# Packed attention in eight array tiles: four heads of 64 rows by 32 columns in place of two pairs of 128 by 64

## The chip, the cores and the metric

The kernel runs on one core of one Trainium2 chip. The metric is the device time of one execution in microseconds, lower is better. A core has TensorE (matmuls into PSUM, an array of 128 rows by 128 columns), VectorE (DVE in the rows), ScalarE (ACT), GpSimd (POOL) and SyncE (SP), which here issues the DMA transfers. PE in the rows is a matmul on TensorE, PEld the load of its stationary operand.

## The reference, cut to what matters

Three layers run in a row on 8 batches of 576 tokens. The change is in the first, a packed attention with 8 heads of 64 features: 32 packed queries `p` attend to the 576 keys and values, and the tokens' queries `q` then attend to the 32 packed values.

```python
def _attn_ref(q, k, v, p):                      # (8, 8, 576, 64), p: (8, 8, 32, 64)
    scale = 1.0 / np.sqrt(q.shape[-1])
    def sm_attn(qq, kk, vv):
        s = scale * np.matmul(qq, kk.transpose(0, 1, 3, 2))
        s = s - np.max(s, axis=-1, keepdims=True)
        a = np.exp(s)
        a = a / (np.sum(a, axis=-1, keepdims=True) + 1e-09)
        return np.matmul(a, vv)
    p_packed = sm_attn(p, k, v)                 # 32 packed values per head
    return sm_attn(q, p_packed, p_packed)
```

Its output `x` (576 x 512 per batch) goes into a mixture of four causal attention experts (`x @ wq[e]`, `x @ wk[e]`, `x @ wv[e]`, the two best experts by `x @ w_gate`), and that into a gated feed-forward layer (`r * (k * k @ w_v)` with `k = relu(xk @ w_k)`, `r = sigmoid(xr @ w_r)`).

## The kernel before, in words

The program has two parts in time. In the first, for each of the 8 batches, two *fronts* compute the packed attention of four heads each (`front(b, g)`, `g` in 0 and 1). The packed attention's output `x` itself is never formed: since `x` is the softmax weights (`A2`) times the packed values, the packed values are multiplied with the experts' weights first (`PW` = packed values times `wa`, 772 columns: queries, keys, values and gate of all experts). `project` and `values` then multiply `A2` and `PW`, each split into a high and a low part (`A2h`, `A2l`, `PWh`, `PWl`). `soft`, `turn` and `pair_out` are the causal attention of the experts. Between them run `fold` and `vweights`, which decode the last layer's weights on VectorE, ScalarE and GpSimd (lines L576 to L617) and multiply some of them on TensorE (L670). In the second part, from about 440 us on, TensorE runs the last layer (`rstage` L801, `kstage` L823, `vstage` L856).

In a front, four heads lie as two pairs. The packed queries of a pair stand in `pT` with zeros beside them (128 rows are two heads' features, 64 columns are two heads' queries, block diagonal), so that a matmul of 128 rows by 64 columns gives both heads' scores. Four such matmuls (two pairs, two halves of 288 tokens) are a call of `scores_pair`, L204, once with the keys `kT` and once with the queries `qT`. The product of weights and values is at L260 (five blocks of tokens, two pairs, 128 value columns), after which `bmask` puts zeros in the wrong head's place (L267). `PW` is at L290. The steps of a front in order are: loads (L223 to L235), key scores and their softmax (L204, L239 to L247), transposes of the weights (L251), product with the values (L260, L267), transposed packed values (L273), query scores (L204, L280 to L285), `PW` (L290 to L297), the rest of the softmax (L300 on) and `A2` (L307).

All matmuls of a front are in float32. Each is two passes in the trace, so a matmul in the program stands there as two loads and two matmul rows.

The order of the work is set twice. A table of due times (`FRONT_T`, `VAL_T`, `SOFT_T` and so on, in units in which a batch takes 20) sorts the pieces into one sequence, in which the generators are advanced. A scheduler then lays the instructions out on each engine by a simulated timeline and the priorities of `PR`. The change alters no due time, but the scheduler's result shifts with the instructions.

Of the kernel before, what the change touches and what calls it, by code (L numbers as in the profile page):

```python
# [9 lines left out]
F32 = mybir.dt.float32  # L10
# [40 lines left out]
def f32(ap):  # L51
    return ap.bitcast(F32)
# [3 lines left out]
def kernel(  # L56
# [3 lines left out]
):  # L60
    nc = tc.nc
    P = 128
    B, NG, _, _, S = q.shape
    D, NPK = p.shape[3], p.shape[5]
    DM, DFF = w_k.shape
    NE, HD = 4, wo.shape[1] // 4
    SH = S // 2
    NT = (S + P - 1) // P
    TAIL = S - (NT - 1) * P
    QB = 256  # L70
# [3 lines left out]
    NCB = S // NPK  # L74
    VG = HD * NE + NE
    NQK = QK + VG
    assert w_in.shape == (DM, NQK) and out.shape[2] == DM == NG * 4 * D
    assert (P, S, D, NPK, HD, NE, NT, TAIL) == (128, 576, 64, 32, 64, 4, 5, 64)
    SC = 1.0 / math.sqrt(D)

# [11 lines left out]
    def nm(s):  # L92
        uid[0] += 1
        return f"{s}_{uid[0]}"
# [12 lines left out]
        out=mstrip[:, 512:], in_=mstrip[:, 512:], pattern=[[-1, P]], base=0,  # L107
        channel_multiplier=1, compare_op=ALU.is_ge, fill=NEG,
    )
    bmask = const.tile([P, 2, D], F32, name="bmask")  # L110
    nc.vector.memset(bmask, 0.0)
    for h in range(4):
        nc.vector.memset(bmask[32 * h : 32 * h + 32, h % 2, :], 1.0)
    lower = const.tile([P, NE, NE], F32, name="lower")
    nc.vector.memset(lower, 0.0)
    for e in range(1, NE):
# [25 lines left out]
    if True:  # L142
# [6 lines left out]
        ex_cm, ex = pool("ex", 2, "left")  # L149
        bt_cm, bt = pool("bt", 1, "left")  # L150

        wa = wa_pool.tile([P, NDT, NQK], F32, name="wa")

# [3 lines left out]
        kls = [ex.tile([P, 2, S], F32R, name=f"kl{x}", bufs=1) for x in range(2)]  # L157
        mss = [ex.tile([P, S], F32, name=f"ms{x}", bufs=1) for x in range(6)]
        vns = [ld.tile([P, NT, 4 * D], F32, name=f"vn{x}", bufs=1) for x in range(2)]
        pTs = [fr.tile([P, P], F32, name=f"pT{x}", bufs=1) for x in range(2)]  # L160
        for t in pTs:
            nc.gpsimd.memset(t, 0.0)

# [14 lines left out]
                yield  # L178

        def load_wa():  # L180
            nc.sync.dma_start(wa, w_in.rearrange("(c p) n -> p c n", p=P))

        def halves(ap):
            return ap.rearrange("p (h n) -> p h n", h=2)
# [12 lines left out]
        def pool_tt(o, x, y, op):  # L197
            nc.gpsimd.tensor_tensor(o, x, y, op=op)  # L198

        def scores_pair(lhs, rhs):  # L200
            ps = big()
            for hf in range(2):
                for jj in range(2):
                    nc.tensor.matmul(  # L204
                        ps[64 * jj : 64 * jj + 64, 512 * hf : 512 * hf + SH],
                        lhs[:, 64 * jj : 64 * jj + 64],
                        rhs[:, jj, SH * hf : SH * hf + SH],
                        start=True, stop=True,
                    )
            return halves(ps)[:, :, :SH]  # L210

        def front(b, g):


            if g == 0:
                bats[b] = {
                    n_: bt.tile([P, NG, w], F32R, tag=n_, name=nm(n_))
                    for n_, w in (("A2h", S), ("A2l", S), ("PWh", NQK), ("PWl", NQK))
                }
            bat = bats[b]  # L220
            pT = pTs[(b * NG + g) % 2]
            for h in range(2):
                nc.sync.dma_start(  # L223
                    pT[64 * h : 64 * h + 64].rearrange("d (j h n) -> d j h n", j=2, h=2)[:, :, h, :],
                    p[b, g, h],
                )
            kT = ld.tile([P, 2, S], F32, tag="kT", name=nm("kT"))
            nc.sync.dma_start(kT, k[b, g])
            vn = vns[(b * NG + g) % 2]
            nc.sync.dma_start(  # L230
                vn[:, : NT - 1, :], v[b, g, : (NT - 1) * P].rearrange("(c p) x -> p c x", p=P)
            )
            nc.sync.dma_start(vn[TAIL:, NT - 1, :], v[b, g, (NT - 1) * P :])
            qT = ld.tile([P, 2, S], F32, tag="qT", name=nm("qT"))
            nc.sync.dma_start(qT, q[b, g])  # L235
            yield
            s1 = scores_pair(pT, kT)
            mx = sm.tile([P, 1], F32, tag="mx1", name=nm("mx1"))
            nc.vector.tensor_reduce(mx, s1, op=ALU.max, axis=AX.XY)  # L239
            nb = sm.tile([P, 1], F32, tag="nb1", name=nm("nb1"))  # L240
            nc.vector.tensor_scalar(nb, mx, -SC, None, op0=ALU.mult)
            a1 = fr.tile([P, S], F32, tag="sa", name=nm("a1"), bufs=4)
            su = sm.tile([P, 1], F32, tag="su1", name=nm("su1"))
            nc.scalar.activation(halves(a1), s1, AF.Exp, bias=nb, scale=SC, accum_out=su)
            nc.vector.tensor_scalar(su, su, EPS, None, op0=ALU.add)
            ri = sm.tile([P, 1], F32, tag="ri1", name=nm("ri1"))
            nc.vector.reciprocal(ri, su)  # L247
            yield
            ps = big()
            for c in range(NT):  # L250
                nc.tensor.transpose(  # L251
                    ps[:, c * P : (c + 1) * P], a1[:, start(c) : start(c) + P], ident
                )
            aT = fr.tile([P, NT, P], F32, tag="aT1", name=nm("aT1"), bufs=1)
            evac(E_AT, aT.rearrange("p c q -> p (c q)"), ps[:, : NT * P])
            yield
            ps = one()
            for c in range(NT):
                for jj in range(2):
                    nc.tensor.matmul(  # L260
                        ps[64 * jj : 64 * jj + 64, :P],
                        aT[:, c, 64 * jj : 64 * jj + 64],
                        vn[:, c, P * jj : P * jj + P],
                        start=c == 0, stop=c == NT - 1,
                    )
            pp = fr.tile([P, P], F32, tag="pp", name=nm("pp"))
            nc.vector.scalar_tensor_tensor(  # L267
                pp, ps[:, :P], ri, bmask.rearrange("p a d -> p (a d)"),
                op0=ALU.mult, op1=ALU.mult,
            )  # L270
            yield
            ps = one()
            nc.tensor.transpose(ps[:, :P], pp, ident)  # L273
            ppT = fr.tile([P, P], F32, tag="ppT", name=nm("ppT"))
            evac(E_PPT, ppT, ps[:, :P])
            yield
            s2 = scores_pair(ppT, qT)
            st = fr.tile([P, S], F32, tag="sa", name=nm("st"), bufs=4)
            for hf in range(2):
                nc.vector.transpose(st[:, SH * hf : SH * hf + SH], s2[:, hf, :])  # L280
            st3 = st.rearrange("p (c n) -> p c n", n=NPK)
            m2 = sm.tile([P, NCB], F32, tag="m2", name=nm("m2"))
            nc.vector.tensor_reduce(m2, st3, op=ALU.max, axis=AX.X)
            pool_tt(st3, st3, m2.unsqueeze(2).to_broadcast([P, NCB, NPK]), ALU.subtract)
            nc.scalar.activation(st, st, AF.Exp, scale=SC)  # L285
            yield
            ps = big()
            for lo, hi in ((0, QK), (QK, NQK)):
                for jj in range(2):
                    nc.tensor.matmul(  # L290
                        ps[64 * jj : 64 * jj + 64, lo:hi],
                        ppT[:, 64 * jj : 64 * jj + 64],
                        wa[:, 2 * g + jj, lo:hi],
                        start=True, stop=True,
                    )
            nc.scalar.copy(bat["PWh"][:, g, :], ps[:, :NQK])
            nc.vector.tensor_sub(bat["PWl"][:, g, :], ps[:, :NQK], f32(bat["PWh"][:, g, :]))  # L297
            yield
            s_ = sm.tile([P, NCB], F32, tag="s2", name=nm("s2"))
            nc.vector.tensor_reduce(s_, st3, op=ALU.add, axis=AX.X)  # L300
            nc.vector.tensor_scalar(s_, s_, EPS, None, op0=ALU.add)
            r_ = sm.tile([P, NCB], F32, tag="r2", name=nm("r2"))
            nc.vector.reciprocal(r_, s_)
            pool_tt(st3, st3, r_.unsqueeze(2).to_broadcast([P, NCB, NPK]), ALU.mult)
            yield
            a2 = fr.tile([P, S], F32, tag="sa", name=nm("a2"), bufs=4)
            nc.vector.transpose(a2, st)  # L307
# [622 lines left out]
def layout(q, k, v, p, moe_w_gate, moe_wq, moe_wk, moe_wv, moe_wo,  # L930
           moe2_mu_k, moe2_mu_r, moe2_w_k, moe2_w_v, moe2_w_r):

    import numpy as np

    b, h, _, d = q.shape
    ne, dm, hd = moe_wq.shape

    def features(a):  # L940
        return a.reshape(b, h // 4, 2, 2, -1, d).transpose(0, 1, 3, 5, 2, 4)

    cols = []
    for e in range(0, ne, 2):
        cols += [moe_wq[e], moe_wq[e + 1], moe_wk[e], moe_wk[e + 1]]
    arrays = {
        "q": features(q).reshape(b, h // 4, 2 * d, 2, -1),
        "k": features(k).reshape(b, h // 4, 2 * d, 2, -1),
        "v": v.reshape(b, h // 4, 4, -1, d).transpose(0, 1, 3, 2, 4).reshape(b, h // 4, -1, 4 * d),
        "p": features(p),  # L950
        "w_in": np.concatenate(cols + list(moe_wv) + [moe_w_gate], axis=1),
        "wo": moe_wo.reshape(ne * hd, dm).T,
        "mu_k": moe2_mu_k, "mu_r": moe2_mu_r, "w_k": moe2_w_k, "w_v": moe2_w_v, "w_r": moe2_w_r,
    }
# [21 lines left out]
```

## Time and profile before

| | us |
|---|---|
| median of 3 runs | 864.74 (861.79 to 866.11) |
| profiled execution | 864.43 |
| its span, first to last instruction | 862.6 |
| TensorE matmuls, busy | 811.9 (94%), 5408 passes |
| VectorE, busy | 569.4 (66%) |
| GpSimd, busy | 397.0 (46%) |
| ScalarE, busy | 369.9 (43%) |

"Busy" is the time in which at least one instruction of the engine ran; a matmul's row holds the time until its last column has left the array, so rows overlap, and a covered stretch isn't TensorE at its peak. The granted clock (PEclk) was 0.985 of full speed over the span. A table of stretches gives each engine's busy time in a window, and the count of instructions that lie in it. A wait is idle time of an engine, put down to what ended it.

### The profile page before, as it was taken

The page shows a single profiled execution, that of the slowest core. Times are in us where ns is not written, and L with a number is a line of the kernel's source. Part 1 is how long each engine was busy: PE and PEld are TensorE (multiplying, and loading weights), DVE is VectorE, ACT ScalarE, POOL GpSimd, SP SyncE. Part 2 cuts the span into 40 slices and gives each one's busy share as a digit, 9 for nine tenths or more (in the row PEclk, how much of TensorE's full clock was granted, in tenths as well). Part 3 has the DMA queues.
Part 4 walks back from the last instruction along what each step waited for, and adds up shares of the span by engine and source line. Part 5 has one row for each costly group of instructions (what it writes and reads, how often), then busy time and mean ns, then how long its engine had stood idle before and what let it go on. Part 6 is the DMA issues. An engine that isn't in the chain of part 4 may idle for free. (4 is left out here: it accounts for less than half of the span.)

```text
span 862.6 us, 15000 instructions
## 1 busy us (share of the span) xinstructions
PE 811.9 (94%) x5408; PEld 676.2 (78%) x5408; DVE 569.4 (66%) x1297; ACT 369.9 (43%) x922; POOL 397.0 (46%) x535
## 2 busy tenths in 40 slices
PE   5799999999999998997999989999999999999998
PEld 3476968779687695776777868988888888898896
DVE  3899696876969789898775774545454544544342
ACT  2347666476655765757666543212112122121120
POOL 6678486483864846445441261333413233232230
PEclk9799999999999999999999989999999999999999
DMA  9764563635546265341546964032121231120301
GB/s 309 243 159 160 144 186 94 197 104 138 171 119 198 87 180 196 98 130 44 163 128 232 348 254 183 1 121 75 49 110 37 87 110 49 74 74 10 137 2 73
DMA packets 65546, 113.71 MB, mean 132 GB/s; under 512 B 9920, under 2 KB 44224, under 8 KB 65472
## 3 DMA queue, kind: packets, MB, share of 16 engines
q1 hardware_dynamic: 65472, 112.75, 40.5%
q8 instruction: 43, 0.70, 0.3%
q14 instruction: 31, 0.25, 0.1%
HBM read 69.74 MB, written 33.55 MB: 120 GB/s over the span
## 5 line engine op out<-in xcount | busy, mean ns | idle before, releaser
L198 POOL TENSOR_TENSOR kk<-y,kk 128x768 fp32r<-128x768 f32 x48 | 89.9, 1873 | 214.1 <-ACT kk L836 214.1
L856 PE MATMUL one<-wvh,kk 128*128 128x512 f32 x576 | 187.6, 393 | 0.1
L856 PEld LDWEIGHTS one<-wvh,kk 128*128 128x128 f32 x576 | 107.6, 188 | 22.6 <-DVE rr L861 0.5
L856 PE MATMUL one<-wvl,kk 128*128 128x512 f32 x288 | 113.2, 394 | 0.0
L466 ACT ACTIVATE ms<-ms,nb 64x64 f32<-64x64 f32 (+4 forms) x160 | 89.4, 559 | 42.4 <-DVE nb L462 40.3
L836 ACT CAST kk<-y 128x768 fp32r<-128x768 f32 x48 | 40.1, 836 | 133.7 <-DVE y L834 97.3
L784 DVE TENSOR_TENSOR y<-big,p 128x256 f32<-128x256 f32 x48 | 20.3, 424 | 116.4 <-POOL kk L198 100.7
L191 ACT COPY tb<-one 64x128 f32<-64x128 f32 (+5 forms) x208 | 66.0, 356 | 21.4 <-PE one L482 19.3
L831 ACT COPY p<-big 128x256 f32<-128x256 f32 x48 | 17.9, 372 | 124.3 <-PE big L823 105.5
L856 PEld LDWEIGHTS one<-wvl,kk 128*128 128x128 f32 x288 | 54.1, 188 | 10.4
L482 PE MATMUL one<-ident,ms 128*128 128x128 f32 x320 | 54.3, 282 | 6.7 <-ACT ms L466 3.6
L462 DVE CUSTOM_DVE_ANT_0 ms<-one,mstrip 64x64 f32<-64x64 f32 (+3 forms) x128 | 51.4, 421 | 9.7 <-PE one L450 7.7
L527 PE MATMUL one<-tb,vg 128*64 128x320 f32 (+4 forms) x448 | 56.1, 361 | 0.9 <-ACT tb L191 0.7
L597 POOL TENSOR_TENSOR dcx<-dcx,dcu 128x256 f32<-128x256 f32 x40 | 30.8, 770 | 45.6 <-DVE dcu L591 18.3
L527 PEld LDWEIGHTS one<-tb,vg 128*64 128x64 f32 x448 | 38.2, 137 | 17.3 <-ACT tb L191 2.7
L482 PEld LDWEIGHTS one<-ident,ms 128*128 128x128 f32 x320 | 37.6, 142 | 17.6 <-issue 7.1
L861 DVE TENSOR_TENSOR rr<-one,rr 128x512 f32<-128x512 f32 x36 | 23.1, 685 | 41.3 <-PE one L856 41.1
L834 DVE SCALAR_TENSOR_TENSOR y<-y 128x768 f32<-128x768 f32 x48 | 47.9, 998 | 1.6
L187 POOL TENSOR_SCALAR dh<-dl 128x2048 fp32r<-128x2048 f32 x10 | 20.9, 2086 | 56.6 <-DMA dl<-dscr 46.6
L779 DVE TENSOR_TENSOR dl<-dl,dh 128x2048 fp32r<-128x2048 f32 x10 | 30.4, 3038 | 19.0 <-POOL dh L187 19.0
L450 PE MATMUL one<-ks,qs 128*128 128x64 f32 (+3 forms) x128 | 39.4, 334 | 3.7 <-DMA ks<-ks 1.9
L823 PE MATMUL big<-dh,wk0h 128*128 128x256 f32 x192 | 39.1, 281 | 1.0 <-DVE rr L786 0.5
(179 smaller groups left out, 2145.5 us busy)
## 6 DMA issues: line engine op xcount, KB each, us to landing
dl<-dscr SPq DMA_DIRECT2D x10, 1024.0 KB, 6.2
kT<-in_k_dram SPq DMA_DIRECT2D x16, 576.0 KB, 4.6
qT<-in_q_dram SPq DMA_DIRECT2D x16, 576.0 KB, 5.6
rscr<-rr SPq DMA_DIRECT2D x12, 768.0 KB, 5.2
rr<-rscr SPq DMA_DIRECT2D x12, 768.0 KB, 4.2
out_dram<-rr SPq DMA_DIRECT2D x11, 768.0 KB, 3.3
vn<-in_v_dram SPq DMA_DIRECT2D x16, 512.0 KB, 4.7
dscr<-dt SPq DMA_DIRECT2D x16, 384.0 KB, 3.6
```

The lines of the kernel that those rows point to most:

```text
L191: nc.scalar.copy(o, x)
L198: nc.gpsimd.tensor_tensor(o, x, y, op=op)
L450: nc.tensor.matmul(ps[:, po : po + kn], qs[:, i * P : i * P + P], keys[:, ko : ko + kn], start=x == 0, stop=x == 1,)
L462: nc.vector.tensor_tensor_reduce(halves(mv) if last else mv, sv, halves(mk) if last else mk, op0=ALU.add, op1=ALU.min, scale=-SC, scalar=3 ...
L466: nc.scalar.activation(mv, mv, AF.Exp, bias=nb[p0:], scale=-1.0, accum_out=bat["sums"][p0:, i, e : e + 1],)
L482: nc.tensor.transpose(ps[:, at + j * P : at + (j + 1) * P], ms[:, j * P : (j + 1) * P], ident)
L527: nc.tensor.matmul(av[64 * ee : 64 * ee + 64, qo - lo : hi - lo], vg[:, j, HD * (2 * ep + ee) : HD * (2 * ep + ee + 1)], tslice(tabs[ee], ...
L597: nc.gpsimd.tensor_add(f32(t["x"]), f32(t["x"]), f32(t["u"]))
L823: nc.tensor.matmul(ps[:, o : o + EB], wpart("k0" if f < 4 else "k1", s, wx, t)[:, f % 4 * P : f % 4 * P + P], dx[:, NS * t + s, :], start= ...
L834: nc.vector.scalar_tensor_tensor(y, y, 0.0, y, op0=ALU.max, op1=ALU.mult)
L836: nc.scalar.copy(kk[:, 0], y)
L856: nc.tensor.matmul(ps, kk[:, a, x, t0 : t0 + P], wres["v"][b][:, f, :], start=n == 0, stop=n == 3 * NFT - 1,)
```

## The change

The four heads of a front get an array tile each way: the array is used as eight tiles of 64 rows by 32 columns. Rows 0 to 63 work on the first half of the tokens (or of the expert columns) and rows 64 to 127 on the second half; each head has its 32 columns. One helper, `heads`, issues the eight matmuls of a call and stands for `scores_pair` and for the loop of `PW`. The inputs are laid out anew for it on the host side of the kernel: `q` and `k` with one half of the tokens on each half of the partitions, `w_in` likewise with one half of its columns, `p` plainly as 64 features by 128 packed queries, which is loaded twice. The packed values are needed on both halves, so the scaling writes them twice, and the zeros (`pTs`, `bmask`) are gone. The product with the values becomes five blocks by four heads, 64 value columns each, in four tiles of 128 rows by 32 columns.

```diff
-        def scores_pair(lhs, rhs):
+        def heads(lhs, rhs, n):
             ps = big()
-            for hf in range(2):
-                for jj in range(2):
+            for h in range(4):
+                for x in range(2):
                     nc.tensor.matmul(
-                        ps[64 * jj : 64 * jj + 64, 512 * hf : 512 * hf + SH],
-                        lhs[:, 64 * jj : 64 * jj + 64],
-                        rhs[:, jj, SH * hf : SH * hf + SH],
+                        ps[32 * h : 32 * h + 32, 512 * x : 512 * x + n],
+                        lhs[64 * x : 64 * x + 64, 32 * h : 32 * h + 32],
+                        rhs[64 * x : 64 * x + 64, h, :],
                         start=True, stop=True,
                     )
-            return halves(ps)[:, :, :SH]
+            return halves(ps)[:, :, :n]
...
-            pT = pTs[(b * NG + g) % 2]
-            for h in range(2):
-                nc.sync.dma_start(
-                    pT[64 * h : 64 * h + 64].rearrange("d (j h n) -> d j h n", j=2, h=2)[:, :, h, :],
-                    p[b, g, h],
-                )
-            kT = ld.tile([P, 2, S], F32, tag="kT", name=nm("kT"))
+            pT = fr.tile([P, P], F32, tag="pT", name=nm("pT"))
+            for x in range(2):
+                nc.sync.dma_start(pT[64 * x : 64 * x + 64], p[b, g])
+            kT = ld.tile([P, 4, SH], F32, tag="kT", name=nm("kT"))
...
-            s1 = scores_pair(pT, kT)
+            s1 = heads(pT, kT, SH)
...
             for c in range(NT):
-                for jj in range(2):
+                for h in range(4):
                     nc.tensor.matmul(
-                        ps[64 * jj : 64 * jj + 64, :P],
-                        aT[:, c, 64 * jj : 64 * jj + 64],
-                        vn[:, c, P * jj : P * jj + P],
+                        ps[32 * h : 32 * h + 32, :D],
+                        aT[:, c, 32 * h : 32 * h + 32],
+                        vn[:, c, D * h : D * h + D],
                         start=c == 0, stop=c == NT - 1,
                     )
             pp = fr.tile([P, P], F32, tag="pp", name=nm("pp"))
-            nc.vector.scalar_tensor_tensor(
-                pp, ps[:, :P], ri, bmask.rearrange("p a d -> p (a d)"),
-                op0=ALU.mult, op1=ALU.mult,
+            nc.vector.tensor_scalar(
+                pp.rearrange("p (x d) -> p x d", x=2),
+                ps[:, :D].unsqueeze(1).to_broadcast([P, 2, D]), ri, None, op0=ALU.mult,
             )
...
-            s2 = scores_pair(ppT, qT)
+            s2 = heads(ppT, qT, SH)
...
-            ps = big()
-            for lo, hi in ((0, QK), (QK, NQK)):
-                for jj in range(2):
-                    nc.tensor.matmul(
-                        ps[64 * jj : 64 * jj + 64, lo:hi],
-                        ppT[:, 64 * jj : 64 * jj + 64],
-                        wa[:, 2 * g + jj, lo:hi],
-                        start=True, stop=True,
-                    )
-            nc.scalar.copy(bat["PWh"][:, g, :], ps[:, :NQK])
-            nc.vector.tensor_sub(bat["PWl"][:, g, :], ps[:, :NQK], f32(bat["PWh"][:, g, :]))
+            ps = heads(ppT, wa[:, 4 * g : 4 * g + 4, :], NQK // 2)
+            nc.scalar.copy(halves(bat["PWh"][:, g, :]), ps)
+            nc.vector.tensor_sub(halves(bat["PWl"][:, g, :]), ps, halves(f32(bat["PWh"][:, g, :])))
```

The order of the instructions moves with it. On VectorE, at the start of the program, before the change (`st` are the transposed query scores of the first two fronts, `m` and `s` their maxima and sums, `dce`, `dcx` and `dcu` steps of a decode of `raw`):

```order
L280 STREAM_TRANSPOSE st_291<-big_286 128x288 x2
L283 TENSOR_REDUCE m_49_294<-st_291 128x18
L267 SCALAR_TENSOR_TENSOR pp_265<-one_254,ri_23_205,bmask 128x128
L582 TENSOR_SCALAR dce_225<-raw_222 128x256
L280 STREAM_TRANSPOSE st_318<-big_313 128x288 x2
L585 SCALAR_TENSOR_TENSOR dcx_224<-raw_222,dce_225 128x256
L300 TENSOR_REDUCE s_59_332<-st_291 128x18
```

And at the same place of the changed program:

```order
L262 TENSOR_SCALAR pp_285<-one_264,ri_25_205 128x128
L569 TENSOR_SCALAR dce_225<-raw_222 128x256
L572 SCALAR_TENSOR_TENSOR dcx_224<-raw_222,dce_225 128x256
L575 TENSOR_SCALAR dce_225<-dcx_224 128x256
L275 STREAM_TRANSPOSE st_315<-big_306 128x288 x2
L578 SCALAR_TENSOR_TENSOR dcu_226<-raw_222,dce_225 128x256
L278 TENSOR_REDUCE m_51_318<-st_315 128x18
```

The first decode has moved ahead of the transpose and the maximum of the first front's query scores, and behind the scaling of the second front's packed values.

On TensorE, in the second batch, before the change (query scores `qT`, softmax of the experts `ks`, `kl`, their turned weights `ms`, and `PW`, named `wa`):

```order
L204 MATMUL big_1548<-qT_926,ppT_1469 64x288 x3
L450 MATMUL one_1527<-ks_1188,qs_118 128x64
L450 MATMUL one_1527<-kl_120,qs_118 128x64
L450 MATMUL one_1527<-ks_1188,qs_118 128x448
L450 MATMUL one_1527<-kl_120,qs_118 128x448
L204 MATMUL big_1548<-qT_926,ppT_1469 64x288
L482 MATMUL one_1538<-ident,ms_126 128x128
```

And in the changed program:

```order
L201 MATMUL big_1664<-qT_1010,ppT_1581 32x288 x3
L437 MATMUL one_1643<-ks_1280,qs_112 128x64
L437 MATMUL one_1643<-kl_114,qs_112 128x64
L437 MATMUL one_1643<-ks_1280,qs_112 128x448
L437 MATMUL one_1643<-kl_114,qs_112 128x448
L201 MATMUL big_1664<-qT_1010,ppT_1581 32x288 x2
L469 MATMUL one_1654<-ident,ms_120 128x128
```

The neighbours are the same; a call of four that was cut into three and one is now a call of eight cut into three, two and three (the last three follow behind the transposes).

## Rows read from the trace of the kernel before

**Rows 1.** The page, busy time, share of the span and instructions of each engine.

```profile
PE 811.9 (94%) x5408; PEld 676.2 (78%) x5408; DVE 569.4 (66%) x1297; ACT 369.9 (43%) x922; POOL 397.0 (46%) x535
```

**Rows 2.** The page, chain that ended last: share of the span by line.

```profile
PE one L856 23%; PE big L823 15%; ACT rr L810 0%; DVE rr L861 0%; DVE y L786 0%; DVE p L785 0%; DVE y L784 0%; ACT p L831 0%
```

**Rows 3.** Table of stretches, all engines; columns in its first row.

```profile
core 0: us, PE busy (x) PEld busy (x) DVE busy (x) ACT busy (x) POOL busy (x), PEclk, DMA share, GB/s
0.00:40.00 40.00, 23.14 (x142) 14.21 (x143) 23.77 (x59) 10.94 (x20) 26.41 (x57) 0.87 0.85 278
40.00:305.00 265.00, 253.81 (x1970) 205.68 (x1970) 212.35 (x616) 165.35 (x482) 176.79 (x302) 0.99 0.51 149
305.00:420.00 115.00, 105.40 (x803) 84.08 (x801) 101.55 (x286) 74.71 (x217) 57.42 (x94) 0.99 0.41 124
...
523.00:862.00 339.00, 334.64 (x2013) 296.20 (x2011) 160.57 (x235) 58.81 (x98) 98.02 (x52) 1.00 0.21 74
```

**Rows 4.** Waits, 40 to 460 us: total us, times, longest us.

```profile
ACT ms L466 <- DVE nb L462: 40.3, 41, 3.0
ACT tb L191 <- PE one L482: 18.2, 23, 2.9
...
PEld one L482 <- ACT ms L466: 6.5, 9, 1.9
...
PE one L482 <- ACT ms L466: 3.6, 3, 1.7
```

**Rows 5.** Line L290: min, median, max ns; first and last start; forms.

```profile
L290 PE MATMUL big<-wa,ppT x128: 382/553/1116, 22.0 to 392.0; 128*64 128x512 f32 x64, 128*64 128x260 f32 x64
```

**Rows 6.** Table of stretches, line L260 alone; columns us, PE, PEld, PEclk, DMA.

```profile
40.00:305.00 265.00, 14.45 (x200) 11.39 (x200) 0.99 0.51 149
305.00:420.00 115.00, 5.25 (x80) 4.29 (x80) 0.99 0.41 124
```

**Rows 7.** Timeline, TensorE: start us, us, line, operands, count of passes.

```profile
18.16 1.26 PE L260 MATMUL one<-vn,aT 128*64 128x128 f32 x20
...
63.17 1.19 PE L204 MATMUL big<-qT,ppT 128*64 128x288 f32 x8
64.19 1.47 PE L290 MATMUL big<-wa,ppT 128*64 128x512 f32 x8
```

**Rows 8.** Table of stretches inside one call: L204, last row L260.

```profile
17.14:17.15 0.01, 0.01 (x2) 0.01 (x2) 1.00 0.00 0
17.15:17.43 0.28, 0.28 (x2) 0.19 (x4) 1.00 1.05 411
...
17.44:17.45 0.01, 0.01 (x4) 0.01 (x2) 1.00 1.27 515
17.14:18.11 0.97, 0.97 (x8) 0.48 (x8) 1.00 1.01 399
...
18.16:19.25 1.09, 1.09 (x20) 1.02 (x20) 1.00 1.01 391
```

**Rows 9.** Groups by line, VectorE: count, busy us, mean ns, idle before.

```profile
L267 DVE SCALAR_TENSOR_TENSOR pp<-one,ri,bmask 128x128 f32<-128x128 f32 x16 | 5.5, 346 | 1.0 <-PE one L260 0.9
```

**Rows 10.** Timeline, start of the program, idle before in brackets.

```profile
2.20 0.60 DVE L113 MEMSET bmask<- 32x64 f32 x4
...
5.53 2.19 PE L204 MATMUL big<-kT,pT 128*64 128x288 f32 x8 [5.53 <-DMA pT<-in_p_dram]
...
18.38 0.85 DVE L280 STREAM_TRANSPOSE st<-big 128x288 f32<-128x288 f32 x2 [1.29 <-PE big L204]
...
21.05 0.77 DVE L582 TENSOR_SCALAR dce<-raw 128x256 int32<-128x256 int32 x1 [0.78 <-DMA raw<-in_w_k_dram]
...
33.06 0.80 PE L332 MATMUL one<-PWh,A2h 128*128 128x260 f32 x2 [1.46 <-POOL A2h L187]
...
36.97 0.85 PE L387 MATMUL big<-A2h,PWh 128*128 128x288 f32 x2
```

More of the change, by code (lines that the diff above doesn't have):

```diff
@@ L62 @@
     P = 128
-    B, NG, _, _, S = q.shape
-    D, NPK = p.shape[3], p.shape[5]
+    B, NG, _, _, SH = q.shape
+    S = 2 * SH
+    D, NPK = p.shape[2], p.shape[3] // 4
     DM, DFF = w_k.shape
     NE, HD = 4, wo.shape[1] // 4
-    SH = S // 2
     NT = (S + P - 1) // P
@@ L76 @@
     NQK = QK + VG
-    assert w_in.shape == (DM, NQK) and out.shape[2] == DM == NG * 4 * D
+    assert w_in.shape == (P, 4 * NG * NQK // 2) and out.shape[2] == DM == NG * 4 * D
     assert (P, S, D, NPK, HD, NE, NT, TAIL) == (128, 576, 64, 32, 64, 4, 5, 64)
@@ L109 @@
     )
[L110 to L113, printed above, removed]
     lower = const.tile([P, NE, NE], F32, name="lower")
@@ L150 @@
         bt_cm, bt = pool("bt", 1, "left")
-        wa = wa_pool.tile([P, NDT, NQK], F32, name="wa")
+        wa = wa_pool.tile([P, 4 * NG, NQK // 2], F32, name="wa")
         qss = [ex.tile([P, TAIL + 2 * S], F32R, name=f"qs{x}", bufs=1) for x in range(2)]
@@ L159 @@
         vns = [ld.tile([P, NT, 4 * D], F32, name=f"vn{x}", bufs=1) for x in range(2)]
-        pTs = [fr.tile([P, P], F32, name=f"pT{x}", bufs=1) for x in range(2)]
-        for t in pTs:
-            nc.gpsimd.memset(t, 0.0)
         for t in vns:
@@ L180, in load_wa @@
         def load_wa():
-            nc.sync.dma_start(wa, w_in.rearrange("(c p) n -> p c n", p=P))
+            nc.sync.dma_start(wa.rearrange("p h n -> p (h n)"), w_in)
         def halves(ap):
@@ L233, in front @@
             nc.sync.dma_start(vn[TAIL:, NT - 1, :], v[b, g, (NT - 1) * P :])
-            qT = ld.tile([P, 2, S], F32, tag="qT", name=nm("qT"))
+            qT = ld.tile([P, 4, SH], F32, tag="qT", name=nm("qT"))
             nc.sync.dma_start(qT, q[b, g])
             yield
-            s1 = scores_pair(pT, kT)
+            s1 = heads(pT, kT, SH)
             mx = sm.tile([P, 1], F32, tag="mx1", name=nm("mx1"))
@@ L940, in features @@
     def features(a):
-        return a.reshape(b, h // 4, 2, 2, -1, d).transpose(0, 1, 3, 5, 2, 4)
+        return a.reshape(b, h // 4, 4, 2, -1, d).transpose(0, 1, 3, 5, 2, 4).reshape(b, h // 4, 2 * d, 4, -1)
     cols = []
@@ L945, in layout @@
         cols += [moe_wq[e], moe_wq[e + 1], moe_wk[e], moe_wk[e + 1]]
+    w_in = np.concatenate(cols + list(moe_wv) + [moe_w_gate], axis=1)
     arrays = {
-        "q": features(q).reshape(b, h // 4, 2 * d, 2, -1),
-        "k": features(k).reshape(b, h // 4, 2 * d, 2, -1),
+        "q": features(q),
+        "k": features(k),
         "v": v.reshape(b, h // 4, 4, -1, d).transpose(0, 1, 3, 2, 4).reshape(b, h // 4, -1, 4 * d),
-        "p": features(p),
-        "w_in": np.concatenate(cols + list(moe_wv) + [moe_w_gate], axis=1),
+        "p": p.reshape(b, h // 4, 4, -1, d).transpose(0, 1, 4, 2, 3).reshape(b, h // 4, d, -1),
+        "w_in": w_in.reshape(h, d, 2, -1).transpose(2, 1, 0, 3).reshape(2 * d, -1),
         "wo": moe_wo.reshape(ne * hd, dm).T,
```

## The prediction

> **What bounds the kernel now.** Read the page's busy shares first, then the chain that ended last, then the table of stretches, then TensorE's waits, and only then the matmuls that the change rewrites. The shares put TensorE at 94% of the span and VectorE at 66% [rows 1], a mean over two programs in a row. From 523 us on, the chain that ended last runs through TensorE's L856 and L823 [rows 2], which the change leaves alone, so I carry that stretch of 339 us over as it is. The changed lines run until 392 us [rows 5]. For them the table of stretches is the view to read [rows 3]: from 40 to 305 us matmuls cover 253.8 of 265 us (96%), while VectorE is busy for 212.35 (80%), GpSimd for 176.8 and ScalarE for 165.4. From 305 to 420 us it is 105.4 of 115 for TensorE (92%), and VectorE has come up to 101.55 (88%). In the list of its waits from 40 to 460 us the longest sum that a matmul waited for another engine is 3.6 us, and that of a weight load 6.5 us, while ScalarE's copies waited 18.2 us for TensorE's transposes [rows 4]. So a microsecond taken off TensorE between 40 and 420 us comes mostly off the time, until VectorE is never free. Before 40 us matmuls cover 23.1 of 40 us and the DMA engines are 85% busy [rows 3]: there the fill of the pipeline sets the pace.
>
> **The change part by part.** There are 16 fronts (8 batches by 2 groups of four heads); each has a score product for the keys, one for the queries, a product of weights and values (20 matmul passes, so the 200 and 80 of [rows 6] are ten fronts between 40 and 305 us and four between 305 and 420 us) and a product with the expert weights. A float32 matmul stands in the trace as two passes, so the four matmuls of a score call are eight rows.
>
> Score products. The four matmuls of 128 rows by 64 columns, over 288 columns each, take 1.19 us at the full clock [rows 7]. The stretches cut out of one call show how [rows 8]: a matmul starts, within 0.01 us a second one, then none for 0.28 us, then two more, and the eight fill 0.97 us before the last tail. So two column tiles run side by side, a pass over 288 columns takes 0.97/4 = 0.242 us, and 0.22 us are first load and tail. Afterwards eight matmuls (16 passes) go to eight tiles of 64 by 32. If these run side by side as the two do, a call is two passes in a row, 0.48 us, with load and tail and some 0.05 us for eight starts 0.75 us: 0.44 us less, twice a front.
>
> Product with the expert weights. Eight passes over 512 and 260 columns take 1.47 us [rows 7]. Afterwards each of eight tiles takes two passes over 386 columns: 2 x 0.242 x 386/288 = 0.65 us, with load, tail and starts 0.91 us: 0.56 us less. The copy and the subtraction behind it handle the same 772 elements a partition, now as two halves in two banks: nothing.
>
> Weights times values. Twenty passes over 128 columns in two tiles take 1.26 us [rows 7], 1.09 us without the tail [rows 8]. Afterwards it is 40 passes over 64 columns in four tiles, ten in a row each. If a pass goes with its columns that is 1.09/2 = 0.55 us, and 0.25 us for starts and tail: 0.80 us, 0.46 us less. This is the least certain of the three, since the instructions double while the data of each halve.
>
> Here a page speaks against the change. The Trainium skill ("TensorEngine Tiling (Array Packing)", Instruction Overhead) states some 60 cycles of overhead for a matmul, so that one over 60 columns costs no less than one over a single column, and advises against taking a tiling factor from a dimension that is already small. No row here has four tiles, so this trace can't say. By that rule 40 passes that queue up for it would take an estimated 1.0 us, and the third saving would be gone.
>
> Sum for TensorE: 0.44 + 0.44 + 0.56 + 0.46 = 1.90 us a front, 19.0 us from 40 to 305 us and 7.6 us from 305 to 420 us. The bounds of what no row shows: 16 passes two at a time, the only overlap in [rows 8], would be 8 x 0.242 = 1.94 us a score call in place of 0.97; all tiles at once is 0.48. I take the second, as the nearer to the row: there a tile with columns of its own doesn't slow its neighbour at all, and eight rest on just that. For the value product the ends are 0.55 and 2.2 us (80 instructions at the pace of the third rival).
>
> How much of it shortens the time. From 40 to 305 us TensorE would fall from 254 to 235 us. VectorE's 212 us would be 86% of a stretch shortened by all of the 19 us, near the 88% that it has later, where TensorE no longer fills its time. So I keep 0.65 of the saving in the first stretch (12.4 us) and 0.4 in the second (3.0 us), where VectorE is already close. Both shares are my choice; their bounds are 0 and 1. What is late next is VectorE's softmax work, which TensorE's transposes then wait for. In the new order about as many calls are cut in two by other matmuls as before, and the projections keep their neighbours, so I cost the moves on TensorE in this stretch at nothing; if the cover is gone, each cut call adds one more load and tail of 0.2 us.
>
> The start. The memsets that go (two on GpSimd, five on VectorE) had ended by 2.8 us, while the first matmul waited until 5.53 us for its packed queries [rows 10]: nothing. Those and the expert weights move the same bytes as before in as many transfers, in longer runs: nothing, within 1 us either way. Scaling the packed values is still 128x128 out of PSUM, 0.346 us [rows 9]; 0.25 to 0.45 us, 16 times, on VectorE. The moved order does matter: VectorE has its first decode (L582 before) ahead of the transpose of the first query scores. That decode ran at 21.05 us, when its data had landed, the transpose at 18.38 us [rows 10], so the first softmax of the queries is 3 to 4 us later. Behind it hang the first value product (33.06 us) and the first projection (36.97 us, [rows 10]). Since VectorE did that decode in between anyway, most of it comes back: with the durations of the rows in the new order I get the projection's operands 1 to 2 us later, against 1 to 2 us from shorter products in the chain. I put the start at 0, with 3 us to either side.
>
> Sum: the profiled execution took 864.4 us (span 862.6 and 1.8 around it; the median of the runs is 864.7). 864.4 - 12.4 - 3.0 = 849.0 us.
>
> **The rivals.** A difference under 0.5% (4.3 us) can't be told from no change.
>
> The second engine takes over. The tiles run as I say, but VectorE and the chain through ScalarE and GpSimd hold the stretch, and a tenth of the 26.6 us is kept: 862 us. For it: VectorE at 80 and 88% [rows 3], ScalarE waiting 40.3 us for VectorE's maxima [rows 4]. Against it: TensorE's own short waits.
>
> Instructions take turns. In the value product 20 loads and 20 matmuls fill 1.09 us [rows 8], 27 ns apiece. If that is the pace of instructions and not of data, a score call of 32 takes 0.87 us instead of 0.97, the expert product 0.87 instead of 1.25, the value product of 80 takes 2.2 instead of 1.1: -0.1 - 0.1 - 0.4 + 1.1 = +0.5 us a front, 14 x 0.5 x 0.65 = 4.5 us, 869 us. If only the value product fails to gain, the time is 14 x 0.46 x 0.6 = 4 us above the forecast, inside its range. Against it: the second tile's matmul starts within 0.01 us of the first [rows 8]. The page named above has a rule of this kind.
>
> Row halves take turns. Four column tiles run side by side, the upper and the lower 64 rows don't: the score calls and the expert product keep their time, and the value product alone gains 4 us: 860.5 us.
>
> The other sign: two tiles at a time is all there is. Nothing in [rows 8] shows three. Then a score call takes 1.94 us (+0.97), the expert product 8 x 0.324 = 2.6 us (+1.3), the value product stays: +3.2 us a front where TensorE sets the pace, 14 x 3.2 x 0.9 = 41 us, so 905 us. It decides as soon as fewer than four tiles overlap.
>
> **How the numbers follow.** Forecast 0.63, with a range of its own from 836 to 860 us; second engine 0.14; instructions in turn 0.08; row halves in turn 0.07; two at a time 0.08. The predicted time is the forecast's, 849 us. For 8 in 10 I go down to 834 us (all of the 26.6 us, and the start 3 us better) and up to 867 us, which takes in the second engine, the row halves and half of the instructions in turn. Faster by over 0.5%: the forecast, half of the row halves, a fifth of the second engine, 0.69. Slower: two at a time and half of the instructions in turn, 0.12. Within 0.5%: the rest, 0.19.
>
> **What would show it.** A key or query score call is one group of 16 passes of about 0.75 us at the full clock, with eight starts in its first tenth of a microsecond; the expert product is near 0.9 us, the value product near 0.8 us. At 1.2 us or more for the last, instructions take turns; at 1.9 us or more for a score call, two tiles at a time is right. The final chain should begin some 15 us before 523 us and last about 339 us as now; VectorE's share between 40 us and the last front should rise by 3 points or more. I am wrong if the groups shrink as forecast and the final chain begins less than 4 us earlier, or if the groups don't shrink.

## The result: the changed kernel is slower, 874.7 us

Four executions of the changed kernel have a median of 874.69 us (872.53 to 877.07), four of the kernel before 865.42 us (861.79 to 866.52). The ratio is 1.0115, 95% interval 1.0072 to 1.0158: slower by some 10 us where I had forecast 15 us less.

The profiled execution took 872.5 us (span 870.7). Its table of stretches, against [rows 3] (the last row is again the 339 us of the final chain, which now begins at 529 us):

```profile
0.00:40.00 40.00, 17.75 (x214) 8.23 (x215) 23.03 (x54) 9.87 (x19) 26.26 (x57) 1.00 0.80 273
40.00:305.00 265.00, 238.13 (x2361) 187.20 (x2360) 216.72 (x596) 159.31 (x460) 172.55 (x291) 0.95 0.50 147
305.00:420.00 115.00, 102.58 (x995) 81.00 (x994) 102.03 (x287) 77.47 (x225) 60.70 (x100) 0.97 0.41 124
531.00:870.00 339.00, 333.50 (x2003) 295.01 (x2002) 160.63 (x235) 58.86 (x98) 98.12 (x52) 1.00 0.20 74
```

The final chain is as long as it was. From 40 to 305 us TensorE is covered for 238 us where it was 254, but the work gets less far: the first projection of the sixth batch starts at 310.2 us instead of 302.5. The hole is idle time, and the granted clock is 0.95 in place of 0.99. The tiles themselves do what was forecast. The timeline has, for calls that no other matmul cuts (before: [rows 7]):

```profile
255.79 0.71 PE L201 MATMUL big<-kT,pT 64*32 64x288 f32 x16
270.41 0.77 PE L254 MATMUL one<-vn,aT 128*32 128x64 f32 x40
296.45 0.88 PE L201 MATMUL big<-wa,ppT 64*32 64x386 f32 x16
```

That is 0.71, 0.77 and 0.88 us where 0.75, 0.80 and 0.91 were forecast and 1.19, 1.26 and 1.47 stood before. So eight tiles run side by side, and so do four.

TensorE's waits from 40 to 460 us show where the time went; before, no matmul waited longer than 2.4 us there (columns as in [rows 4]):

```profile
PE one L476 <- DVE nb L449: 9.7, 5, 6.1
PE one L469 <- DVE nb L449: 6.4, 2, 5.4
PE one L476 <- DVE cb L531: 3.4, 3, 1.6
```

Two waits of 5.4 and 6.1 us for VectorE's maxima (`nb`) stand out. Around the first, the timeline of all engines reads:

```profile
118.90 2.03 POOL L181 TENSOR_SCALAR wh<-wc 128x256 fp32r<-128x256 f32 x4
119.20 0.74 DVE L278 TENSOR_REDUCE m<-st 128x18 f32<-128x576 f32 x1
119.86 0.28 DVE L575 TENSOR_SCALAR dce<-dcx 128x256 int32<-128x256 int32 x1
...
120.71 6.31 DVE L569 TENSOR_SCALAR dce<-raw 128x256 int32<-128x256 int32 x1
120.91 0.72 POOL L669 TENSOR_TENSOR oo<-oo 128x256 f32<-128x256 f32 x1
...
121.60 1.15 POOL L192 TENSOR_TENSOR st<-st,m 128x576 f32<-128x576 f32 x1
...
122.71 0.71 POOL L584 TENSOR_TENSOR dcx<-dcx,dcu 128x256 f32<-128x256 f32 x1
...
123.43 2.75 POOL L604 TENSOR_TENSOR wl<-wc,wh 128x256 fp32r<-128x256 f32 x4
126.15 0.72 POOL L670 TENSOR_TENSOR oo<-oo 128x256 f32<-128x256 f32 x1
127.05 0.23 DVE L449 CUSTOM_DVE_ANT_0 ms<-one,mstrip 64x64 f32<-64x64 f32 x1
...
128.09 1.09 PE L469 MATMUL one<-ident,ms 128*128 128x128 f32 x4 [5.39 <-DVE nb L449]
```

One decode step of VectorE, usually 0.28 to 0.34 us long, lasts 6.31 us: as long as GpSimd works without a pause beside it, on operations with two inputs (and one memset of 0.09 us between them). The maxima that TensorE's transposes need stand behind it in VectorE's queue. The Trainium skill ("SBUF — State Buffer", SBUF: two separate sides) says that VectorE and GpSimd share one pair of ports as an exclusive lock, contended by VectorE's two-port fast modes and, against reads by GpSimd, by its operations with two SBUF inputs, and that the one that starts first holds it for its whole instruction. This trace agrees in that VectorE is shut out, but the instruction did not wait for one GpSimd instruction: it waited for the whole run of them. The step has one input, and no row shows whether it ran in such a mode.

The start moved too: the first projection at 43.37 us instead of 36.97 [rows 10].

```profile
43.37 0.43 PE L374 MATMUL big<-A2h,PWh 128*128 128x288 f32 x2
```

### The profile page after: what moved, and what is told of

Its sections match the earlier page's. It is cut to its first block, busy times and chain, and to the rows that moved or that the text cites. A ratio compares the mean times of both kernels' runs of the same rounds, so it can differ in the third digit from the quotient of the medians.

```text
span 870.7 us, 16388 instructions
## 1 busy us (share of the span) xinstructions
PE 792.6 (91%) x6112; PEld 652.5 (75%) x6112; DVE 579.4 (67%) x1292; ACT 370.4 (43%) x922; POOL 397.9 (46%) x533
## 5 line engine op out<-in xcount | busy, mean ns | idle before, releaser
L771 DVE TENSOR_TENSOR y<-big,p 128x256 f32<-128x256 f32 x48 | 20.3, 424 | 116.0 <-POOL kk L192 100.3
L469 PE MATMUL one<-ident,ms 128*128 128x128 f32 x320 | 54.3, 284 | 9.2 <-DVE nb L449 6.4
L514 PE MATMUL one<-tb,vg 128*64 128x320 f32 (+4 forms) x448 | 59.0, 374 | 2.1 <-DVE nb L449 1.8
L514 PEld LDWEIGHTS one<-tb,vg 128*64 128x64 f32 x448 | 36.3, 140 | 25.9 <-issue 4.8
L476 PE MATMUL one<-ident,ms 128*128 128x128 f32 x160 | 35.7, 285 | 15.4 <-DVE nb L449 9.7
L181 POOL TENSOR_SCALAR dh<-dl 128x2048 fp32r<-128x2048 f32 x10 | 20.9, 2087 | 57.1 <-DMA dl<-dscr 47.3
```

What stands on the lines that cost most here:

```text
L469: nc.tensor.transpose(ps[:, at + j * P : at + (j + 1) * P], ms[:, j * P : (j + 1) * P], ident)
L476: nc.tensor.transpose(pd[:, at + P * x : at + P * x + P], ms[:, start(i) : start(i) + P], ident)
L514: nc.tensor.matmul(av[64 * ee : 64 * ee + 64, qo - lo : hi - lo], vg[:, j, HD * (2 * ep + ee) : HD * (2 * ep + ee + 1)], tslice(tabs[ee], ...
```

## The experiments

The change does two things at once: it packs the tiles, and it makes the scheduler lay out every engine anew. Most runs below take these apart. Ratios are to the kernel before, run beside them; 0.01 is 8.6 us.

**Tiles and order apart.** A table (written out per engine from one kernel's program) and one call at the end of the other kernel (with marks that count the program's steps), which ties each instruction behind the one before it in the table on its engine:

```diff
+ORDERS = {"PE": "...", "Activation": "...", "DVE": "...", "Pool": "...", "SP": "..."}
...
         close(cms["bb"], cms["ba"], cms["bk"])
+        impose(tc, nc, marks)
```

> The changed kernel's instructions, each engine made to take them in the order of the kernel before. Theory A (the packed tiles are worth most of what was forecast, and the moved order lost it): 845 to 855 us, no TensorE gap over 3 us between 40 and 440 us, the first projection near 37 us and the final chain begins by 512 us. Theory B (TensorE's time sets little here, so neither costs nor gains): 861 to 868 us, the final chain begins at 520 to 525 us. Theory C (the loss goes with the packed tiles themselves, since an emptier TensorE falls to half clock more often): 870 us or more, with as much half clock as in the changed kernel.

Measured: 861.95 us, ratio 0.9986 (0.9966 to 1.0007).

> The kernel before, each engine made to take its instructions in the order of the changed kernel. Theory A: the new order costs what it cost there and nothing is saved: 882 to 895 us, with TensorE gaps of 5 us or more at the same two places. Theory B: the order alone, with TensorE's time beside the point: 871 to 878 us. Theory C: 861 to 868 us, since the loss stays with the packed tiles.

Measured: 880.79 us, ratio 1.0208 (1.0173 to 1.0243). So the loss is the order's, 11 us with the tiles (1.0115 against 0.9986) and 18 us without, as theory A has it, and C falls. But the tiles gain only 1 us in the old order (the interval includes nothing at all) and 8 us in the new one, which is B; the second time lies between the ranges of A and B. In the second run VectorE's long step comes back, in a kernel without a single packed tile, and TensorE waits 4.5 us behind it; a second wait of 5 us, which A forecast, is not there:

```profile
123.28 6.30 DVE L718 TENSOR_SCALAR dce<-raw 128x256 int32<-128x256 int32 x1
129.61 0.23 DVE L598 CUSTOM_DVE_ANT_0 ms<-one,mstrip 64x64 f32<-64x64 f32 x1
```

**The collisions alone.** In the new order four VectorE instructions out of 1125 are moved (numbers are steps of the program; 204 is the decode step of 120.7 us, the moved parts of 207 and 216 are the small sum, reciprocal and product of the second wait, the rest are the maxima and transposes between):

```diff
- ... 199x2 204 127x2 129x3 130x2 136 131 135 142x2 ...
+ ... 199x2 127x2 129x3 130x2 136 131 135 204 142x2 ...
- ... 208x2 207 216 207 216 207 213 216 213 214 216 ...
+ ... 208x2 207 216x2 213x2 214 207x2 216x2 ...
```

> The changed kernel in its own order but for four instructions of VectorE: one decode step (the one that took 6.3 us at 120.7 us) now stands behind the five maxima that followed it, and the small sum, reciprocal and product of 185.9 to 188.2 us behind the three maxima there. Theory A1 (those instructions wait for GpSimd's two-input work and hold up the maxima that TensorE waits for; the maxima themselves were never longer than usual beside GpSimd): both TensorE gaps over 5 us fall under 2.5 us, the final chain begins 4 to 9 us earlier than in the changed kernel, 0.990 to 0.996 of its time, so 1.002 to 1.007 of the kernel before. Rival E (the place of these four is beside the point, the rest of the order sets it): 1.009 to 1.014.

Measured: 868.83 us, ratio 1.0071 (1.0049 to 1.0093).

> The unpacked kernel in the new order (1.021 of the kernel before) with the same four instructions moved. Theory A1: 1.011 to 1.017. Rival E: 1.018 to 1.024.

Measured: 870.74 us, ratio 1.0093 (1.0067 to 1.0119). Four instructions give back 4 us with the tiles (1.0115 to 1.0071, just at the edge of what A1 gave) and 10 us without. In the timeline of the kernel with the tiles VectorE's maxima now run beside the same work of GpSimd at their usual length, and the decode step waits alone behind them:

```profile
121.75 0.23 DVE L585 CUSTOM_DVE_ANT_0 ms<-one,mstrip 64x64 f32<-64x64 f32 x1
...
122.02 0.62 DVE L585 CUSTOM_DVE_ANT_0 ms<-one,mstrip 128x448 f32<-128x448 f32 x1
...
126.05 0.75 DVE L585 CUSTOM_DVE_ANT_0 ms<-big,mstrip 128x576 f32<-128x576 f32 x1
...
126.72 2.62 DVE L705 TENSOR_SCALAR dce<-raw 128x256 int32<-128x256 int32 x1
```

Neither of the two long waits is left, and the final chain begins at 523.1 us instead of 529.2, and without the tiles at 526.9 instead of 535.8. Some 7 to 8 us of the new order's cost remain in both, which I did not take apart.

**GpSimd's and VectorE's load.** The same instructions in the same order, on fewer columns (`NP` for GpSimd and `NV` for VectorE are 32); the tiles that are then only partly written are zeroed once at the start. These kernels leave out most of the fold of the weights, and the last three only GpSimd's share of it.

```diff
-            nc.gpsimd.tensor_sub(l, x, f32(h))
+            nc.gpsimd.tensor_sub(l[:, :NP], x[:, :NP], f32(h)[:, :NP])
...
-                t["e"], hi, 3, 0x3FFFFFF8, op0=ALU.logical_shift_left, op1=ALU.bitwise_and
+                t["e"][:, :NV], hi[:, :NV], 3, 0x3FFFFFF8, op0=ALU.logical_shift_left, op1=ALU.bitwise_and
```

> The kernel before in its own order, but the decoding of the weights on VectorE and the fold's work on GpSimd handle 32 columns where there were 256: the same instructions, most of that work left out. Theory B (VectorE and GpSimd behind it set the pace up to 420 us as much as TensorE does): TensorE's idle time from 40 us to the final chain falls from 29 us to 15 or less, so 845 to 852 us. Rival D (the order itself and the waits along the softmax chain set it, whatever VectorE's load): 856 to 863 us.

Measured: 837.07 us, ratio 0.9659 (0.9629 to 0.9689), below even theory B's range; TensorE's idle time is 14.8 us.

> The packed tiles in the old order, with the same decoding and fold work left out as in the run before this one. Theory B: now TensorE alone sets the pace, so nearly all of the 20 us and more that the tiles take off it shows: 15 to 22 us less than the unpacked kernel with the same work left out. Rival D: no more than 6 us less.

Measured: 826.17 us, ratio 0.9545 (0.9499 to 0.9590), so 9.8 us less (0.0114): between the two theories.

> The packed tiles in the old order, with the fold's work on GpSimd alone cut from 256 to 32 columns; VectorE decodes all. If VectorE is held up by GpSimd at what they share: VectorE's instructions lose most of the time by which they are longer than usual before 420 us, and the time falls 8 us or more below that of the packed kernel in the old order (862). If VectorE's own load is what counts: less than 4 us.

Measured: 842.90 us, ratio 0.9721 (0.9684 to 0.9759), 23 us below the packed kernel in the old order. What VectorE's instructions take above the usual of their form (the median of those that no GpSimd instruction overlaps), summed from 40 to 420 us, falls from 42 to 24 us: less than half of it goes, not most.

> The kernel before in its own order with the fold's work on GpSimd alone cut from 256 to 32 columns. If GpSimd's hold on VectorE takes part in the pace even there: 852 to 858 us, a smaller gain than the packed kernel has from the same cut, since TensorE is next. If not: 860 to 865 us.

Measured: 847.56 us, ratio 0.9780 (0.9739 to 0.9820): 19 us from GpSimd's work alone, more than expected, though GpSimd is busy for 46% of the span [rows 1]. The tables of stretches, from 40 us to the start of the final chain, before and in this run:

```profile
40.00:522.40 482.40, 453.53 (x3252) 365.26 (x3252) 385.10 (x1004) 299.54 (x805) 272.61 (x427) 0.99 0.52 161
40.00:502.10 462.10, 444.35 (x3243) 359.05 (x3243) 364.35 (x998) 298.02 (x802) 205.97 (x423) 1.00 0.54 167
```

Of the 20 us by which the chain begins earlier, 11 are idle time of TensorE, and some 6 are the half clock, of which none is left. Theory B holds in this: the engines behind the softmax set the pace up to 420 us as well as TensorE. How GpSimd does so is not taken apart: VectorE's instructions take 17 us less above their usual length (43 to 26 us from 40 to 420 us), but VectorE's idle time that a result of GpSimd ended falls as well, from 27.3 to 12.7 us up to the final chain.

> The changed kernel in its own (new) order, with the fold's work on GpSimd cut from 256 to 32 columns. Theory A1 (the new order is slower because it sets VectorE's decoding beside long runs of GpSimd): the two TensorE gaps over 5 us go, VectorE's 6 us instruction near 121 us is back under 1 us, and the time comes within 4 us of the packed kernel with the same cut in the old order (843). Rival E (it is the rest of the new order, its later start and the place of the softmax steps): it stays 8 us or more above that, at 851 us or more.

Measured: 847.04 us, ratio 0.9798 (0.9768 to 0.9827). Both long waits are gone, and in the profiled execution the final chain begins at 502.4 us, with the new order, against 502.5 us with the old, although the first projection is still late (43.7 against 35.2 us). In the timed runs 6.6 us remain between the orders (0.9798 against 0.9721) where 11 were: most of A1, a rest for E.

**All the work done, GpSimd relieved.** The weights' high part is copied on ScalarE; in the last of the four the high part of the query attention too.

```diff
-E_WH, E_SQ, E_B, E_G, E_CXL = "P", "A", "V", "V", "A"
+E_WH, E_SQ, E_B, E_G, E_CXL = "A", "A", "V", "V", "A"
...
-            pool_copy(bat["A2h"][:, g, :], a2)
+            nc.scalar.copy(bat["A2h"][:, g, :], a2)
```

> The changed kernel with the 84 copies of the weights' high part (0.43 us each) on ScalarE instead of GpSimd, all work done, in the order that this gives by itself. If GpSimd's hold on VectorE is what counts, some 36 us less of it before 420 us give 6 to 12 us: 862 to 868 us against the changed kernel's 874. If ScalarE, which TensorE's transposes wait for, pays for it: no gain, 873 us or more.

Measured: 858.37 us, ratio 0.9933 (0.9904 to 0.9962).

> The kernel before with the same copies on ScalarE, in the order that this gives by itself. If GpSimd's hold counts: 853 to 860 us. If ScalarE pays: 865 us or more. Any order is a draw of its own, so 5 us to either side are in it.

Measured: 869.41 us, ratio 1.0066 (1.0046 to 1.0087): no gain, the second of the two cases. That it is ScalarE that pays doesn't follow, since the next run has the same copies there.

> The packed tiles with those copies on ScalarE, in the order of the unpacked kernel with them there (the run before this one). Packing against no packing in one order again: if TensorE's saving shows the more the less GpSimd holds VectorE, 2 to 6 us less than the unpacked one; if the order and the half clock eat it as in the first order, within 2 us.

Measured: 856.87 us, ratio 0.9929 (0.9898 to 0.9959). In this order the tiles gain 11.8 us, more than either case had. This kernel and the one of 858 us beat both kernels of the case.

> The changed kernel with the weights' high-part copies on ScalarE, as in the run that took 858 us, and also the 16 copies of the query attention's high part (128x576, about 1 us each on GpSimd) on ScalarE; the order is what this gives by itself. If GpSimd's hold on VectorE still costs: 851 to 857 us. If ScalarE, or a worse order, pays: 858 us or more.

Measured: 866.40 us, ratio 1.0028 (1.0006 to 1.0051): less work on GpSimd again, and yet 8 us slower than without the second edit. It is no steady gain. Each edit draws another order; that the order is what cost here is not shown, since no run has the second edit in the order of the first.

**The half clock.** Matmuls on constants, ahead of transposes that had waited:

```diff
             ps = one()
+            for _ in range(FILL.get((b, e, group), 0)):
+                nc.tensor.matmul(ps, ident, mstrip[:, :512], start=True, stop=True)
```

> The packed tiles in the old order (862 us, 0.9986 of the kernel before) with seven idle matmuls of 512 columns added, each ahead of a transpose that TensorE waited 0.9 to 1.8 us for there, so that it is not idle in those waits. Theory C2 (part of the saving goes because an emptier TensorE falls to half clock, 29.5 us of it after 40 us): at least 15 us of the half clock go, and the time falls by 3 us or more, to 0.995 of the kernel before or less. Rival F (the half clock only fills time in which TensorE would wait anyway): the same time as without the added matmuls within 2 us, or up to 6 us more, since each added matmul can take 0.9 us.

Measured: 859.70 us, ratio 0.9942 (0.9916 to 0.9968).

> The packed tiles in the old order with the fold's work on GpSimd cut to 32 columns (842.9 us, 0.972 of the kernel before), and two such idle matmuls ahead of each of the three transposes that waited 1.6 to 2.2 us there. Theory C2: the half clock at 213 and 319 us goes, and with it 5 us or more of the time: 0.966 or less. Rival F: 0.970 to 0.976.

Measured: 845.69 us, ratio 0.9782 (0.9751 to 0.9813), slower than either theory had it. Its timeline shows why neither run settles the question:

```profile
213.10 2.41 PE L627 MATMUL one<-mstrip,ident 128*128 128x512 f32 x4 [2.21 <-DVE nb L609]
```

The added matmuls themselves wait for VectorE's maxima, which, as I take it, still read the PSUM bank that they write. So they ran behind the wait and not in it, at all three places here and at four of the seven of the first run. In this run the half clock of the profiled execution fell from 30.7 to 20.5 us all the same, and the time did not fall with it. The first run gained 4 us (0.9942 against 0.9986), and its profiled execution was at half clock for 10 us after 40 us instead of 29.5; but over its timed executions the mean granted clock was 0.981, against 0.979 without the added matmuls, so I don't put the gain down to the clock.

**The account.** For pairs with one order, from the profiled executions: TensorE's busy time from 40 us to the start of the final chain, its idle time there, the time after 40 us at 1.2 GHz instead of 2.4, and the time of the pair by the ratios.

| pair (without tiles, with tiles) | busy, us | idle, us | half clock, us | chain begins, us | time, us |
|---|---|---|---|---|---|
| old order | 453.5, 439.1 | 28.9, 39.6 | 13.7, 29.5 | 522.4, 518.7 | -1.2 |
| new order | 462.2, 439.6 | 33.6, 49.6 | 26.5, 30.7 | 535.8, 529.2 | -8.0 |
| new order, repaired | 460.2, 440.0 | 26.8, 43.0 | 22.9, 24.2 | 526.9, 523.1 | -1.9 |
| high part on ScalarE | 454.3, 434.3 | 29.7, 40.8 | 20.5, 20.5 | 523.9, 515.1 | -11.8 |
| GpSimd's fold small | 444.3, 433.6 | 17.8, 29.0 | 0, 30.7 | 502.1, 502.5 | -5.1 |
| fold and decode small | 439.1, 422.3 | 14.8, 21.4 | 0, 10.2 | 493.9, 483.7 | -9.8 |

Counting what ran at half clock at its full-clock length, the tiles take 22.0, 21.1, 20.3, 20.0, 25.5 and 21.6 us off TensorE, nearly the same in five of the six pairs. Idle time takes 6.6 to 16.2 us of that back, the half clock from nothing up to 14.8 us (in the fifth pair all that was left). Where VectorE and GpSimd are lightest, the least turns into idle time. The busy, idle and clock columns rest on one execution each, and the times on all: in the fifth pair the two profiled executions lie 0.9 us apart and the medians 4.7. The lower clock with the tiles, though, is there over the timed executions too: a mean of 0.979 against 0.987 in the old order, and 0.978 against 0.993 with GpSimd's fold small.

## Why the prediction was wrong, step by step

**The tiles: right in kind, a fifth too large in sum.** Each of the three calls came within 0.04 us of its forecast. The rivals by which tiles or row halves take turns are out: a score call would have been at 1.2 us or more. So is the one by which instructions take turns, with its 2.2 us for a value product. Over the 14 fronts TensorE's time fell by 20 to 22 us in five of the six pairs and not by 26.6. The calls are not to blame: the rows of the four rewritten products alone, at full-clock length, cover 77.2 us from 40 us on before and 47.3 us with the tiles in the old order, 29.9 us less, and 29 to 31 us less in every pair. But the other matmuls' rows cover 385.3 us there instead of 381.2, and the overlap of the two shrinks from 11.3 to 7.4 us. Taking the difference of the calls alone was the error; why the others' rows grew stays open. The Trainium skill ("TensorEngine Tiling (Array Packing)", Instruction Overhead) has some 60 cycles of overhead for a matmul. By an estimate from that the 40 passes of a value product would fill 1.0 us; the row has 0.77 us with load and tail, so in four tiles that cost does not add up.

**"I keep 0.65 of the saving in the first stretch and 0.4 in the second": failed.** In the old order 1.2 us of the forecast 15.4 us came off the time (0.9966 to 1.0007 of it, so not clear of none), and 1.2 to 11.8 us over the pairs with all the work done. I had taken a TensorE that is covered for 96% of a stretch as the engine that sets the pace. The run with GpSimd's work cut shows otherwise: 19 us went although not one matmul was changed. When its own work gets shorter, TensorE waits for the other engines instead: from before to the tiles in the old order, idle time that a result of VectorE ended rises from 17.5 to 25.6 us, and ScalarE's share from 7.4 to 9.8 us. A second part went to the clock, for which the prediction has no term: in the old order's pair 10.7 us of the saving turn into idle time and some 7.5 us into half clock, by the profiled executions. That the time would have been shorter without the half clock no run shows. The rival "the second engine takes over" had the wait for the other engines, at 862 us, which is what the packed tiles take in the old order; I gave it 0.14. Its number is met closely by luck, since it left out the clock. And I looked for VectorE's pace in its busy share, and it is not there alone: some 43 us of that busy time before, from 40 to 420 us, are instructions that last longer than usual.

**"I cost the moves on TensorE in this stretch at nothing": failed, and decided the sign.** I looked at TensorE's neighbours alone. VectorE's queue was what counted: the new order costs 11 us with the tiles and 18 us without them, and four instructions in it 4 and 10 us. Order and tiles together: -1 + 11 = +10 us, the measured result. By the prediction's own sign it was wrong: the groups shrank as forecast, and the final chain began 7 us later.

**The start, "0, with 3 us to either side": failed as a step.** The first projection came 6.4 us late, and it is the order: 36.3 us with the tiles in the old order, 45.7 us without them in the new one. By the second batch 2.6 us of it were left, and with GpSimd's fold small the final chain began at the same time in both orders, though in the timed runs 6.6 us remained between them.

**What held.** The final chain lasted its 339 us, as said. That the memsets and the loads at the start cost nothing fits the first matmul, which begins at 5.2 us with the tiles in the old order, against 5.5 us before (6.0 us in the changed kernel, where the keys' transfer is issued behind the packed queries'). But the loads were misread: the packed queries' two transfers a front are of 32 KB each and not 16, since each half of the rows gets all four heads. The sign that I had named for the forecast, VectorE's share up by 3 points, did not come: from 40 to 305 us it rose by 1.7 points (80.1 to 81.8%).

## What to carry to other kernels

An engine that is covered for 96% of a stretch need not set its pace: ask what the other engines' instructions last against the usual of their form, since a stretched instruction counts as busy. When an edit makes a scheduler lay out the program anew, run the new instructions in the old order and the old ones in the new order before judging the edit; here one set of instructions with the tiles took 0.999 to 1.012 of the kernel before, and one without them 1.000 to 1.021, by the order alone. In the queue of an engine that another one can hold up, put the work that others wait for ahead of the instructions that can be held.

## What the runs showed of the hardware

VectorE's instructions fall into two kinds beside GpSimd. Over the two kernels' first 530 us, those that read PSUM, the reductions, the transposes and the reciprocals kept their length whatever GpSimd did (the maximum over 128x448 took 0.62 to 0.63 us in all 64 cases, 45 of them with GpSimd at work). Most TENSOR_SCALAR, COPY and two-input forms on SBUF alone did not (some short ones did: two TENSOR_SCALAR of 128x1 elements took 0.10 to 0.16 us in all 64 cases). The decode's first step took 0.31 us on the mean in the 6 cases beside an idle GpSimd, and beside its two-input work 0.66 us on the mean and 6.31 us at most; a product of 128x10 elements that takes 0.16 us lasted 3.76 us once. So the longest stalls are as long as GpSimd's run without a pause, and not as one of its instructions. What ends one differs: with the four instructions moved, the decode step ended at 129.34 us, behind GpSimd's last two-input instruction (until 129.12), while GpSimd went on with one-input work; the 128x10 product, with two inputs of its own, ended at 191.94 us, when one-input work of GpSimd ended too (191.92). These are single cases.

An order that is fixed on every engine does not fix the clock. In 12 executions of the packed kernel in the old order the mean granted clock lay between 0.970 and 0.986, with times from 858.5 to 865.3 us.
